# A streamed-weight ring of four buffers instead of five, one more weight block kept resident, and a new order of a step's groups, in a recurrent attention kernel

## The chip, the cores and the metric

The kernel runs on one core of one Trainium2 chip. The metric is the device time of one execution in microseconds (us). The kernel before has a median of 2057.08 us over three runs, from 2056.86 to 2064.43.

## The reference

Two branches read the same `x` of 2048 x 640 and are mixed by a gate.

```python
# branch A: attention with a window of 256 keys, 32 heads of 20
# branch B: 64 segments of 32 tokens, one after the other
for s in range(n_seg):
    h = concatenate([mem, x[segment s]])          # 8 + 32 = 40 tokens of 640
    q = einsum('btd,dhe->bhte', h, Wq)            # 32 heads of 192
    k = einsum('btd,dhe->bhte', h, Wk)
    v = einsum('btd,dhe->bhte', h, Wv)
    p = softmax(mask(q k^T * scale))
    o = einsum('bhte,hed->btd', p v, Wo)
    mem = o[:, :8, :]                             # the next segment needs this
    outs.append(o[:, 8:, :])
return g * a + (1 - g) * b                        # g = sigmoid(x . gate_w)
```

Branch B is a recurrence: segment s+1 needs the first eight rows of segment s. Each of its four weights has 640 x 6144 elements of two bytes, so all four together are read once per segment and don't fit into the on-chip memory at once.

## The kernel before

The kernel computes branch A first (to about 300 us), then what branch B can compute for all segments together, then 64 steps, one for each segment. The steps are what the change touches.

A step works on four groups of eight heads. For each group there are the projections q, k and v, the transposes tq and tk, the scores s, the transposed probabilities p, the values pv and two halves oa and ob of the output projection. `m` turns the new memory rows at the end. `STEP` is the order in which TensorE does them:

```python
STEP = ("k0 q0 k1 tk0 tq0 q1 s0 tk1 q2 tq1 k2 v0 p0 s1 tq2 q3 k3 pv0 tk2 v1 p1 s2 oa0 tq3 tk3 ob0 pv1 v2 p2 s3 oa1 ob1 pv2 v3 p3 "
        "oa2 pv3 ob2 oa3 ob3 m")
```

The weights are cut into 84 blocks: five for each of q, k and v in each group (128 rows of 1536 elements, 384 KB), six for o in each group (128 rows of 1280 elements, 320 KB). Most stay in on-chip memory for the whole run ("resident"). The others are fetched from HBM anew in each step ("streamed"), into a ring of buffers of 1536 elements a row:

```python
RING = 5
STREAMED = {"q": ((1,), (1,), (2,), (1,)),        # for each group, which of its blocks are streamed
            "k": ((0,), (3,), (3,), (3,)),
            "v": ((4,), (0, 4), (0, 3), (3,)),
            "o": ((2,), (2, 5), (0, 3), (2, 5))}
...
ring = wctx.enter_context(tc.tile_pool(name="b_w", bufs=RING))
```

A projection of a group takes its five blocks one after the other, four matmuls for each. A streamed block is one DMA issued from SyncE:

```python
def chunk(kind, s, g):
    ...
    wb = pieces(kind, g)                          # the streamed blocks: a ring buffer and a load each
    def f(kt):
        w = w_of(kind, g, kt, wb)
        for j in range(4):
            nc.tensor.matmul(t[32 * j:32 * j + 32, 0:384], lhsT=tile_of(hT)[:, kt, :], rhs=w[:, j * 384:(j + 1) * 384], ...)
    for kt in range(KT):
        sc.op("PE", 160, 330, lambda kt=kt: f(kt), reads=[hT] + [wb[m] for m in wb if m == kt], ...)
```

The output projection does the same with its blocks, three in oa and three in ob. SyncE issues the loads in the order in which TensorE uses the blocks. The load of block n writes the buffer that block n-5 had, so it waits until TensorE has done the four matmuls of block n-5; a matmul on a streamed block waits for its load.

What is not streamed is loaded once, ahead of the steps:

```python
resident = [...every block that is not streamed...]
early, late, last = resident[:EARLY], resident[EARLY:-LAST], resident[-LAST:]   # EARLY = 24, LAST = 11
```

`early` is loaded during branch A, `late` during the stage between, `last` into buffers that come free before or just after the first step begins.

Of the kernel before, what the change touches and what calls it, by code (L numbers as in the profile page):

```python
# [608 lines left out]
def pe_order(nseg):  # L609

    names = [(w.rstrip("0123456789"), w.lstrip("abcdefghijklmnopqrstuvwxyz")) for w in STEP.split()]
    return [(k, s) + ((int(g),) if g else ()) for s in range(nseg) for k, g in names]


STEP = ("k0 q0 k1 tk0 tq0 q1 s0 tk1 q2 tq1 k2 v0 p0 s1 tq2 q3 k3 pv0 tk2 v1 p1 s2 oa0 tq3 tk3 ob0 pv1 v2 p2 s3 oa1 ob1 pv2 v3 p3 "
        "oa2 pv3 ob2 oa3 ob3 m")


KEPT = {"QT": (1, [P, 12 * L + 64 - L]), "Kz": (1, [P, 4, 2, L]), "Px": (2, [P, 64]), "PTx0": (1, [P, 2, 4, 2, MEM]), "PTx1": (1, [P, 2, 4, 2, MEM]),
# [50 lines left out]
def branch_B(ctx, tc, xin, mem0, weights, ring, c, omg_sb, ga_dram, b_dram, outf, hold, held, rest):  # L670
# [6 lines left out]
    sb = {  # L677
        "w": (RING, [P, PIECE]), "tok": (3, [P, 384]), "vtok": (1, [P, 384]), "K02": (1, [P, 4, 2, L]),
        "PTm": (1, [P, 2, 4, L]), "Pm": (1, [P, 4, SEG]), "xg": (2, [P, 2, 12, MEM]), "xv": (1, [P, 384]), "hT": (2, [P, KT, SEG]),
# [354 lines left out]
    with tc.manual_schedule():  # L1034
        parts = []
        for n in names:
# [10 lines left out]

PARTS = {"oa": range(3), "ob": range(3, 6)}
TURNS = (range(2), range(2, KT))
RING = 5  # L1050
EARLY = 24
LAST = 11
HOLD = 5
DENSE = 8
STREAMED = {"q": ((1,), (1,), (2,), (1,)),
            "k": ((0,), (3,), (3,), (3,)),
            "v": ((4,), (0, 4), (0, 3), (3,)),
            "o": ((2,), (2, 5), (0, 3), (2, 5))}


@with_exitstack
def kernel(
# [31 lines left out]
    allp = [(k, g, m) for k in KINDS for g in range(4) for m in range(6 if k == "o" else 5)]  # L1094
    streamed = [(k, g, m) for k, g, m in allp if m in STREAMED[k][g]]
    weights = Weights(tc, B_Wq, B_Wk, B_Wv, B_Wo, streamed)
# [6 lines left out]
    units = [lambda u=u: weights.load_resident(pre, u, nc.sync) for u in early]  # L1103
    ring = wctx.enter_context(tc.tile_pool(name="b_w", bufs=RING))
    first = {}
# [122 lines left out]
```

## Time and profile before

| what | value |
|---|---|
| median of three runs | 2057.08 us |
| span of the profiled execution | 2060.6 us |
| TensorE matmul busy | 1918.0 us, 93% of the span |
| VectorE, ScalarE, GpSimd busy | 50%, 46%, 35% |
| moved by DMA | 593.83 MB, mean 288 GB/s |
| the step's end (line 977), first to last of 64 | 463.3 to 2052.4 us |
| from issue to landing of a streamed block, least, median, most | 3.3, 4.9, 8.3 us |

The last row but one gives the length of a step: (2052.4 - 463.3) / 63 = 25.22 us. In the profile, PE is TensorE's matmul stream and SP is SyncE, which issues the weight loads. `b_w` is a ring buffer, `w_q`, `w_k`, `w_v`, `w_o` and `hold` are resident blocks, and `in_B_Wq_dram` and the like are the weights in HBM. "Landing" is the moment at which the semaphore of a DMA says that its data is there. In the table of waits, each row is one line of the kernel, what it waited for, the total time in us, how many times, and the longest. A row of a stretch gives the busy time of each engine in it, the granted TensorE clock, the mean busy share of the 16 DMA engines, and the rate in GB/s.

### The profile page before, as it was taken

What the parts mean: (1) busy time and instruction counts of PE and PEld (TensorE: products, weight loads), DVE (VectorE), ACT (ScalarE), POOL (GpSimd) and SP (SyncE); (2) the same over time, 40 slices, a digit from 0 to 9 for tenths busy, and PEclk for the clock granted to TensorE, in tenths of its full rate; (3) what the DMA queues carried; (4) which work ended last, traced back from release to release, by engine and by line L of the source; (5) the groups of instructions that cost most, each with busy time, mean ns of one, the idle gap of its engine ahead of it and who ended that gap; (6) DMA issues with size and microseconds to landing.
All of it is one profiled execution on the core that took longest, in us unless ns stands there. A gap on an engine that the chain in (4) does not pass through costs nothing. (4 is left out here: it accounts for less than half of the span.)

```text
span 2060.6 us, 92206 instructions
## 1 busy us (share of the span) xinstructions
PE 1918.0 (93%) x39670; PEld 1411.6 (69%) x39670; DVE 1027.7 (50%) x3337; ACT 947.3 (46%) x1949; POOL 717.4 (35%) x2008
## 2 busy tenths in 40 slices
PE   7999999989999999999999999999999999999997
PEld 6878878756666666666666666766666666666665
DVE  4888853334444444444444444544444444444444
ACT  3888832334444444444444444444444444444443
POOL 4221121233333333333333333433333333333332
PEclk9999999999999999999999999999999999999999
DMA  4222149789999999999999999999999999999997
GB/s 138 86 82 70 45 99 353 204 271 339 330 327 335 324 334 334 328 328 338 335 329 333 329 327 324 336 321 329 319 337 331 335 334 319 338 332 332 337 329 256
DMA packets 251153, 593.83 MB, mean 288 GB/s; under 512 B 39528, under 2 KB 59120, under 8 KB 250736
## 3 DMA queue, kind: packets, MB, share of 16 engines
q1 hardware_dynamic: 219248, 540.07, 75.2%
q0 software_dynamic: 31488, 47.78, 8.6%
q8 instruction: 313, 5.13, 1.0%
q14 instruction: 104, 0.85, 0.1%
HBM read 558.33 MB, written 29.37 MB: 285 GB/s over the span
## 5 line engine op out<-in xcount | busy, mean ns | idle before, releaser
L773 PEld LDWEIGHTS <-b_hT 128*32 128x32 bf16 x15360 | 374.7, 96 | 261.4 <-issue 65.5
L968 PEld LDWEIGHTS <-b_OT 128*64 128x64 bf16 x6144 | 371.9, 110 | 59.9 <-issue 36.9
L773 PE MATMUL ps_q<-w_q,b_hT 128*32 128x384 bf16 x4096 | 257.6, 329 | 1.6 <-issue 1.6
L773 PE MATMUL ps_k<-w_k,b_hT 128*32 128x384 bf16 x4096 | 246.0, 329 | 0.0
L968 PE MATMUL ps_o<-hold,b_OT 128*64 128x320 bf16 x2560 | 236.5, 300 | 0.0
L968 PE MATMUL ps_o<-b_w,b_OT 128*64 128x320 bf16 x1792 | 206.5, 301 | 26.6 <-DMA b_w<-in_B_Wo_dram 24.5
L919 DVE TENSOR_TENSOR b_PTm<-PT_ps,marks 128x320 bf16<-128x320 f32 x256 | 125.9, 492 | 207.6 <-PE PT_ps L907 207.6
L824 DVE TENSOR_TENSOR b_Kz<-tr_k,marks 128x256 bf16<-128x256 bf16 x256 | 108.0, 422 | 221.2 <-PE tr_k L797 217.2
L773 PE MATMUL ps_v<-w_v,b_hT 128*32 128x384 bf16 x3584 | 212.8, 327 | 0.0
L946 ACT CAST b_OT<-ps_pv 128x480 bf16<-128x480 f32 x256 | 142.9, 558 | 144.9 <-PE ps_pv L942 144.9
L239 ACT ACTIVATE pt<-s_ps 128x1024 bf16<-128x1024 f32 x180 | 183.5, 1025 | 55.2 <-PE s_ps L236 52.0
L784 ACT CAST b_tok<-ps_k 128x384 bf16<-128x384 f32 x256 | 122.4, 478 | 166.2 <-PE ps_k L773 157.6
L784 ACT CAST b_vtok<-ps_v 128x384 bf16<-128x384 f32 x256 | 122.5, 478 | 158.4 <-PE ps_v L773 156.6
L718 POOL DMA_DIRECT2D b_xg<-xin x256 | 141.9, 554 | 83.5 <-POOL b_QT L810 51.4
L968 PE MATMUL ps_o<-w_o,b_OT 128*64 128x320 bf16 x1792 | 170.6, 300 | 0.2 <-ACT b_vtok L784 0.2
L829 POOL COPY b_K<-b_xg 128x64 bf16<-128x64 bf16 x256 | 60.5, 236 | 312.7 <-PE S_ps L853 309.4
L784 ACT CAST b_tok<-ps_q 128x384 bf16<-128x384 f32 x256 | 122.9, 480 | 91.3 <-PE ps_q L773 90.8
L806 ACT COPY b_QT<-tr_q 128x384 bf16<-128x384 bf16 x256 | 123.3, 482 | 85.0 <-PE tr_q L797 85.0
L773 PE MATMUL ps_v<-b_w,b_hT 128*32 128x384 bf16 x1536 | 131.7, 331 | 29.2 <-DMA b_w<-in_B_Wv_dram 28.1
L997 DVE CAST b_hT<-mem_ps 128x16 bf16<-128x16 f32 x126 | 22.5, 178 | 267.6 <-PE mem_ps L991 264.3
L1013 POOL DMA_DIRECT2D out_dram<-b_ga x128 | 63.5, 496 | 246.8 <-DVE b_ga L1009 237.3
L797 PEld LDWEIGHTS <-b_tok 128*64 128x64 bf16 x3072 | 108.2, 110 | 41.6 <-issue 23.3
(141 smaller groups left out, 3720.7 us busy)
## 6 DMA issues: line engine op xcount, KB each, us to landing
b_w<-in_B_Wv_dram SPq DMA_DIRECT2D x384, 384.0 KB, 4.9
b_w<-in_B_Wo_dram SPq DMA_DIRECT2D x448, 320.0 KB, 4.8
b_w<-in_B_Wk_dram SPq DMA_DIRECT2D x256, 384.0 KB, 5.1
b_w<-in_B_Wq_dram SPq DMA_DIRECT2D x256, 384.0 KB, 5.1
xin<-hold POOLq DMA_DIRECT2D x8, 1536.0 KB, 12.2
b_xg<-xin POOLq DMA_DIRECT2D x256, 48.0 KB, 4.5
w_q<-in_B_Wq_dram SPq DMA_DIRECT2D x16, 384.0 KB, 4.3
w_k<-in_B_Wk_dram SPq DMA_DIRECT2D x16, 384.0 KB, 3.7
```

Of the source, the lines that this page charges most:

```text
L239: nc.scalar.activation(out=pt, in_=sp[:], func=ACT.Exp, scale=scale)
L718: sc.op("POOL", 540, 5000, lambda: nc.gpsimd.dma_start(tile_of(b)[:].rearrange("p i b t -> p (i b t)"), xin[s, :, c:c + 192]), writes=[b])
L773: nc.tensor.matmul(t[32 * j:32 * j + 32, 0:384], lhsT=tile_of(hT)[:, kt, :], rhs=w[:, j * 384:(j + 1) * 384], start=(kt == 0), stop=(kt == ...
L784: nc.scalar.copy(dst, src)
L797: nc.tensor.transpose(t[64 * a:64 * a + 64, k, :], tok["tile"][:, c:c + 64], ident[:], tile_position=(0, 64 * a))
L806: nc.scalar.copy(dst, tq["tile"][:].rearrange("p b (j t) -> p b j t", t=SEG))
L824: nc.vector.tensor_tensor(out=tile_of(Kz)[:, :, :, 0:SEG], in0=src, in1=mk_z.unsqueeze(1).unsqueeze(3).to_broadcast([P, 4, 2, SEG]), op=AL ...
L829: nc.gpsimd.tensor_copy(tile_of(K02)[:, :, :, SEG:L], src[:, :, 0::2, :])
L919: nc.vector.tensor_tensor(out=tile_of(PTm)[:], in0=src.to_broadcast([P, 2, 4, L]), in1=mk_m.unsqueeze(1).unsqueeze(3).to_broadcast([P, 2, ...
L946: sc.op("ACT", 560, 50, lambda: nc.scalar.copy(tile_of(OT)[:, 0:12 * L], o["tile"][:, 0:12 * L]), reads=[o], writes=[OT])
L968: nc.tensor.matmul(t[64 * h:64 * h + 64, 0:D // 2], lhsT=OT["tile"][:, c:c + 64], rhs=w, start=(g == 0 and m == 0 and n == 0), stop=(g == ...
L1013: sc.op("POOL", 500, 3000, lambda h=h: nc.gpsimd.dma_start(half(outf, h), mine(tile_of(ga), h)), reads=[ga])
```

## The change

One ring buffer is given up, and in its room one more block is kept resident. So 20 blocks are streamed in a step instead of 21: 13 of q, k and v (before: 14) and 7 of o (as before). Which blocks are streamed is chosen anew, and TensorE does the parts of a step in a new order. The parts themselves are the same. The aim is to read less from HBM in each step without needing more on-chip memory.

```diff
-STEP = ("k0 q0 k1 tk0 tq0 q1 s0 tk1 q2 tq1 k2 v0 p0 s1 tq2 q3 k3 pv0 tk2 v1 p1 s2 oa0 tq3 tk3 ob0 pv1 v2 p2 s3 oa1 ob1 pv2 v3 p3 "
-        "oa2 pv3 ob2 oa3 ob3 m")
+STEP = ("k0 q0 q1 tk0 tq0 k1 s0 tq1 v0 tk1 k2 q2 p0 s1 q3 tk2 pv0 tq2 k3 v1 p1 s2 tq3 oa0 "
+        "tk3 pv1 ob0 v2 p2 s3 oa1 pv2 v3 ob1 p3 oa2 pv3 ob2 oa3 ob3 m")
...
-RING = 5
+RING = 4
...
-STREAMED = {"q": ((1,), (1,), (2,), (1,)),
-            "k": ((0,), (3,), (3,), (3,)),
-            "v": ((4,), (0, 4), (0, 3), (3,)),
-            "o": ((2,), (2, 5), (0, 3), (2, 5))}
+STREAMED = {"q": ((2,), (3,), (3,), (1,)),
+            "k": ((0,), (2,), (3,), (0,)),
+            "v": ((2,), (3,), (3,), (0, 4)),
+            "o": ((0, 3), (0,), (0, 3), (0, 5))}
```

## The prediction, made before the changed kernel ran

> **What bounds the kernel now.** I read first the table of stretches, for the steady part of the 64 steps, then TensorE's waits in the same stretch, then the DMA issues, then the timeline around one load.
>
> ```profile
> core 0: us, PE busy (x) PEld busy (x) DVE busy (x) ACT busy (x) POOL busy (x), PEclk, DMA share, GB/s
> 950.00:1950.00 1000.00, 933.06 (x20866) 668.66 (x20860) 469.97 (x1709) 436.60 (x992) 382.22 (x1112) 1.00 0.96 330
> ```
>
> TensorE is busy 93% at full clock, and the 16 DMA engines 96%. No other engine reaches half. Two resources run close together, so the waits must say which one holds.
>
> ```profile
> engine line waited for: us in total, times, longest us
> PE mem_ps L991 <- ACT b_OT L977: 22.7, 39, 0.8
> PE ps_v L773 <- DMA b_w<-in_B_Wv_dram: 18.9, 35, 1.4
> PE ps_o L968 <- DMA b_w<-in_B_Wo_dram: 10.1, 26, 1.1
> PE ps_k L773 <- DMA b_w<-in_B_Wk_dram: 4.4, 6, 1.3
> PE ps_q L773 <- DMA b_w<-in_B_Wq_dram: 2.8, 6, 1.4
> ```
>
> The first row is the recurrence, once a step, and the change doesn't touch it. The other four are streamed weights that came late: 36.2 us in 1000 / 25.22 = 39.65 steps, 0.9 us a step. This is a lower bound, because modelled ends of matmuls hide part of a wait. So I took the distance from the start of each part to the start of the next in all steps of the trace, and compared its mean with its 5th percentile, which is the pace without a wait. The undisturbed step is **23.33 us**; the real one is 25.22. Of the 1.9 us between them, 1.58 stand in front of streamed blocks and 0.33 elsewhere. Late weights are the only thing that a change of streaming can win back.
>
> ```profile
> b_w<-in_B_Wv_dram SPq DMA_DIRECT2D x237, 384.0 KB, 4.9
> b_w<-in_B_Wo_dram SPq DMA_DIRECT2D x279, 320.0 KB, 4.7
> b_w<-in_B_Wq_dram SPq DMA_DIRECT2D x159, 384.0 KB, 5.2
> b_w<-in_B_Wk_dram SPq DMA_DIRECT2D x158, 384.0 KB, 5.1
> ```
>
> A load takes some 5 us from issue to landing (mean of all, one by one: 4.97). The timeline shows when a load is issued:
>
> ```profile
> 1001.33 0.34 PE L773 MATMUL ps_q<-b_w,b_hT 128*32 128x384 bf16 x4
> ...
> 1001.72 1.46 SPq L517 DMA_DIRECT2D b_w<-in_B_Wv_dram  x2
> ```
>
> The four matmuls end at 1001.67, and 0.05 us later SyncE issues the next load into a freed buffer. This holds at all 21 places of the step: the issue comes 0.04 us after the end of the use five blocks earlier. SyncE never has a free buffer, so **the ring sets when loads start**. A buffer's cycle is 0.04 (issue) + 4.97 (load) + 0.61 (the block lies ready) + 0.38 (use) = 6.0 us, and indeed 21 blocks x 6.0 / 5 buffers = 25.2 us.
>
> **What the skill says.** The Trainium skill, "DMA: Bandwidth & Descriptors", section "Anatomy of one DMA", gives a transfer a fixed part of about 2.0 us, mostly the confirmation of the last byte. The trace has more than this to explain: in the mean the first row of a block starts 2.27 us after the issue, its 128 rows take 1.19 us, and it lands 1.52 us later. A small store in a quiet stretch started its first row after 0.82 us, so some 1.45 us of the load are a queue. The same page, "Issuing engines are not separate DMA queues", says that all queues share the same 16 engines; the trace agrees, with GpSimd's small transfers, of 20 to 96 KB, landing only after 4.4 to 5.1 us at the median. "Perfetto Trace Analysis", section "Optimization Strategy", says that the same gap coming back on the engine that should be saturated can mean too few buffers. Here that is so already with five.
>
> **The change, part by part.**
>
> *Traffic.* A step streams 14 x 384 + 7 x 320 = 7616 KB before and 13 x 384 + 7 x 320 = 7232 KB after. The DMA engines are busy 0.96 x 25.22 = 24.2 us a step, of which the weight queue has a share of 87.7% of the span, 22.1 us. One block is 22.1 x 384 / 7616 = 1.11 us. The DMA engines' work falls from 24.2 to **23.1 us a step**. If DMA throughput were all, and the share stayed 0.96, the step would be 23.1 / 0.96 = 24.1 us.
>
> *New order.* The TensorE parts are the same and the number of changes between the 32-wide and the 64-wide tiles is too: eight stretches of each kind in both orders, and a change costs about 0.1 us. The distances that evacuations need stay long enough. The shortest new one is p2 to pv2 with s3 and oa1 between: 0.06 + 0.33 + 3 x 0.27 = 1.2 us, while VectorE's two products behind p end 0.96 us after its start (1000.48 to 1001.44 in the timeline). So 0 us, and the undisturbed step stays 23.33.
>
> *The ring.* For each streamed block I count its lead: from the end of the use of the block that had its buffer to its own first matmul, at the undisturbed pace (0.162 us a piece of q, k or v, 0.271 of o, both from the timeline). Before, with five buffers: mean 5.18, least 3.98. After, with four: mean 4.29, in order of the step 4.5 4.5 4.7 4.5 4.5 4.7 4.5 4.4 4.4 4.4 4.5 4.7 4.6 4.2 4.3 3.6 3.5 3.7 3.4 4.1. The new places are spread more evenly, but the o blocks at the end have 3.4 to 3.7 us only. A load that takes longer than its lead stops TensorE for the difference, and each stop lengthens the leads of the blocks around it. Walking through the steps with one constant load time gives the stop per step:
>
> | load time, us | 4.0 | 4.2 | 4.3 | 4.4 | 4.5 | 4.6 | 5.0 |
> |---|---|---|---|---|---|---|---|
> | before, 5 buffers | 0.06 | 0.26 | 0.36 | 0.46 | 0.58 | 0.78 | 1.58 |
> | after, 4 buffers | 0.65 | 0.93 | 1.13 | 1.41 | 1.76 | 2.16 | 3.77 |
>
> The row of before meets the trace: at 5.0 us it says 1.58, and 1.58 was measured in front of streamed blocks at a mean load of 4.97. With four buffers the same stop, so the same time as now, comes at a load of 4.45 us. **The change pays only if a load becomes at least 0.5 us shorter.**
>
> *How long a load takes with four buffers.* The 1.45 us of queue can shrink. Sorted by how much weight data stood ahead of a load when it reached the DMA engines, the trace has 4.23 us with less than half a block ahead (26 loads), 4.89 with about 1.1 and 5.57 with about 1.85: 0.93 us for each block ahead, and 1.17 blocks ahead in the mean. One buffer less takes at most one block out of this queue: 4.97 - 0.93 = 4.04 us. If only half of it is felt, because TensorE's pace and not the queue gives way, it is 4.5. I take the middle, **4.27 us**; between the columns of 4.2 and 4.3 this is a stop of 1.07 us. The step is then 23.33 + 0.33 + 1.07 = 24.73 us, 0.49 less than now; times 64 that is 31 us.
>
> *Outside the steps.* The additional resident block is loaded once, about 1.1 us of the DMA engines, and in the stretch of 360 to 440 us their share is 0.71. 0 to 1 us. The sum: 2057 - 31 = **2026 us**.
>
> **The rivals.**
>
> 1. *The latency doesn't give way.* For it: loads issued while only two others were under way still took 4.9 us against 5.1 with four, a weak dependence. If a load keeps 4.97 us, the stop is 3.65 us, the step 27.3 and the time some 2190. Against it: the DMA engines are 96% busy and over a microsecond of the load is waiting in line, which needs loads ahead to wait for.
> 2. *The queue vanishes wholly and TensorE becomes the bound.* For it: the leads are even, and traffic falls by 5% as well. At 4.04 us the stop is 0.69, the step 24.35, the time 2001. Against it: engines whose queue is short run dry now and then, so the share can't stay at 0.96.
> 3. *The new order costs TensorE a wait*, such as pv2 behind VectorE. 0.2 us a step would be 13 us. The trace shows hardly a wait of this kind now.
>
> **Range and chances.** Loads of 4.04 and 4.5 us give 2001 and, with a step of 25.42, about 2070. These are the ends of the range, a little widened for the walk's error below. Faster by over 2% needs a step under 24.58, a load of about 4.2, just under my middle: 0.34. Slower by over 2% needs 4.62 us or rival 3 on top of a long load: 0.13. The rest is within 2%.
>
> **What would show it.** In the changed profile the landing of weights should read 4.1 to 4.4 us at the median. The DMA share in the steps should be 0.92 to 0.95, against 0.96. TensorE's waits should move from v to the o blocks at the step's end, where the leads are shortest. The recurrence should stay at about 0.57 us a step. Landings still near 4.9 would show rival 1, waits on VectorE in pv rival 3. The weakest step is the load time: 0.1 us of it is 0.2 to 0.4 us a step.

## The result, and the profile after

The changed kernel has a median of 2136.96 us over four runs (2123.07 to 2141.07), against 2058.67 us of the kernel before in the same runs: a ratio of 1.0365, 95% interval 1.032 to 1.041. It is 3.65% slower; 2026 us and a range up to 2070 were predicted. The profiled execution is the shortest of the four, and its steps tell where the time went: their end comes at 463.9 us for the first time and at 2113.1 for the 64th, so a step takes (2113.1 - 463.9) / 63 = **26.18 us** instead of 25.22. The part ahead of the steps is as long as before.

The row of the steady stretch, with the columns as before (busy time of each engine, clock, DMA share, GB/s):

```profile
950.00:1950.00 1000.00, 908.39 (x20097) 635.02 (x20096) 448.96 (x1644) 425.93 (x955) 367.65 (x1071) 1.00 0.92 303
```

TensorE is less busy, 91% instead of 93%, and the DMA engines have room, 0.92 instead of 0.96. Both resources became idler and the step longer. That is what waiting for a latency looks like. TensorE's waits in this stretch (line, what it waited for, total us, times, longest):

```profile
PE ps_v L773 <- DMA b_w<-in_B_Wv_dram: 24.0, 45, 1.4
PE mem_ps L991 <- ACT b_OT L977: 21.7, 38, 0.6
PE ps_q L773 <- DMA b_w<-in_B_Wq_dram: 18.9, 30, 1.6
PE ps_o L968 <- DMA b_w<-in_B_Wo_dram: 13.7, 29, 1.3
PE PT_ps L905 <- DVE b_Pm L883: 5.3, 24, 0.4
PE ps_k L773 <- DMA b_w<-in_B_Wk_dram: 3.5, 6, 1.3
```

Late weights cost 24.0 + 18.9 + 13.7 + 3.5 = 60.1 us in 38.2 steps, 1.6 us a step, where it was 0.9. The recurrence (second row) is unchanged. A wait of the transposed probabilities on VectorE is new. The loads themselves did get shorter, as the DMA issues show (last column: median us from issue to landing):

```profile
b_w<-in_B_Wo_dram SPq DMA_DIRECT2D x266, 320.0 KB, 4.2
b_w<-in_B_Wv_dram SPq DMA_DIRECT2D x190, 384.0 KB, 4.3
b_w<-in_B_Wq_dram SPq DMA_DIRECT2D x154, 384.0 KB, 4.6
b_w<-in_B_Wk_dram SPq DMA_DIRECT2D x152, 384.0 KB, 4.3
```

They were 4.7 to 5.2 us. The mean of all, one by one, fell from 4.97 to 4.38 us; 4.27 was predicted. So the load time came out nearly as expected and the time didn't. The experiments ask why.

### The profile page after: what moved, and what is told of

It reads as the page before. It is cut to its first block, busy times and chain, and to the rows that moved or that the text cites. A ratio compares the mean times of both kernels' runs of the same rounds, so it can differ in the third digit from the quotient of the medians.

```text
span 2121.3 us, 91957 instructions
## 1 busy us (share of the span) xinstructions
PE 1932.7 (91%) x39670; PEld 1395.8 (66%) x39670; DVE 1022.2 (48%) x3337; ACT 957.6 (45%) x1949; POOL 717.6 (34%) x2008
## 3 DMA queue, kind: packets, MB, share of 16 engines
q8 instruction: 313, 5.13, 1.0%
## 4 chain that ended last, share of the span: by engine, by line
PE 49%; DMA 41%; DVE 5%; ACT 3%; issue 2%; SPq 0%; POOL 0%; ACTq 0%; POOLq 0%
DMA b_w<-in_B_Wv_dram 14%; DMA b_w<-in_B_Wo_dram 11%; PE ps_o L968 11%; DMA b_w<-in_B_Wq_dram 10%; PE ps_k L773 6%; PE ps_q L773 6%; PE ps_v L773 4%; PE t_psum L584 4%; DMA b_w<-in_B_Wk_dram 3%; PE qk_ps L138 3%; PE t_psv L602 2%; PE tr_k L797 2%; PE s_ps L236 2%; PE S_ps L853 1%; DVE pt L241 1%
## 5 line engine op out<-in xcount | busy, mean ns | idle before, releaser
L968 PEld LDWEIGHTS <-b_OT 128*64 128x64 bf16 x6144 | 359.7, 110 | 71.6 <-issue 42.7
L773 PE MATMUL ps_q<-w_q,b_hT 128*32 128x384 bf16 x4096 | 244.7, 327 | 0.0
L773 PE MATMUL ps_v<-w_v,b_hT 128*32 128x384 bf16 x3840 | 234.1, 327 | 0.0
L773 PE MATMUL ps_k<-w_k,b_hT 128*32 128x384 bf16 x4096 | 234.0, 328 | 0.0
L968 PE MATMUL ps_o<-b_w,b_OT 128*64 128x320 bf16 x1792 | 207.2, 302 | 24.8 <-DMA b_w<-in_B_Wo_dram 24.1
L968 PE MATMUL ps_o<-hold,b_OT 128*64 128x320 bf16 x2560 | 223.5, 301 | 0.0
L773 PE MATMUL ps_v<-b_w,b_hT 128*32 128x384 bf16 x1280 | 109.5, 331 | 47.2 <-DMA b_w<-in_B_Wv_dram 45.7
L873 DVE TENSOR_REDUCE sm<-S_ps 128x4 f32<-128x160 f32 x256 | 82.3, 322 | 121.0 <-ACT S_ps L870 121.0
```

The lines of the kernel that those rows point to most:

```text
L873: nc.vector.tensor_reduce(out=x["sum"][:], in_=view(), axis=AX.X, op=ALU.add)
L968: nc.tensor.matmul(t[64 * h:64 * h + 64, 0:D // 2], lhsT=OT["tile"][:, c:c + 64], rhs=w, start=(g == 0 and m == 0 and n == 0), stop=(g == ...
```

## The experiments

Theory A: what binds is the time of a load against its lead, the room that the ring gives it. Rivals: B, the new order and choice of blocks; C, the throughput of the DMA engines.

### Four buffers alone

```diff
-RING = 5
+RING = 4
```

> The kernel before with four ring buffers and nothing else: its old order, its 21 streamed blocks. Theory A (the ring: the load time and its scatter against the leads, which fall to about 4.1 us): the walk gives a stop of 2.8 to 3.7 us a step at constant loads of 4.4 to 4.6 us, and scatter adds about 1 us, so a step of 27.5 to 28.5 us and 2200 to 2270 us in all, ratio 1.07 to 1.10. Theory B (the new order and choice of blocks cost the time, not the ring): within 15 us of the kernel before. Theory C (DMA throughput: 24.2 us of DMA engine time a step at the share of 0.92 seen with four buffers): a step of 26.3 us, some 2130 us. The landing at the median should be 4.3 to 4.5 us in A.

Measured: 2202.98 us, the mean of 2192.75 and 2213.25, against 2060.16 of before on the same chip, a ratio of 1.069; two further executions (2226.16 and 2231.78 us) were in a slower state with a lower granted clock and are left out. The profiled execution is that of 2213.25 us, with a step of 27.61 us and a DMA share of 0.91. The landing is 4.4 us at the median. This is the low end of A's range. B as the only cause falls: the ring by itself costs 27.61 - 25.22 = 2.39 us a step. C's 2130 us is too low.

### The changed kernel with five buffers

```diff
-RING = 4
+RING = 5
+ALIAS = {('v', 3, 3): ('v', 3, 2)}     # this resident block is left out, its neighbour is read in its place
```

> The changed kernel with five buffers: new order, new choice, 20 streamed blocks. The room for the fifth buffer comes from leaving one resident v block of the last group out, whose matmuls read the neighbouring block instead, so the work of TensorE and the streamed traffic are those of the changed kernel. Theory A: leads rise to 5.4 us, loads of 4.7 to 4.9 us, a stop of 0.3 to 0.9 us, a step of 24.1 to 24.6 us and 1985 to 2020 us in all. Theory B: still slower than before, 2110 to 2135 us. Theory C: 23.1 to 24.1 us of DMA engine time at a share of 0.96, a step of 24.1 to 25.1 us, 1985 to 2050 us.

Measured: 2003.4 us, ratio 0.9703 (0.966 to 0.9745), a step of 24.30 us. This is within the ranges of A and C, and B is out. It isn't a replacement, as it leaves a block of weights out to make room for the fifth buffer. But it shows the parts of the change apart:

| step, us | 21 blocks, old order and choice | 20 blocks, new order and choice |
|---|---|---|
| 5 buffers | 25.22 | 24.30 |
| 4 buffers | 27.61 | 26.18 |

One block less with the new order and choice is worth 0.92 us with five buffers and 1.43 with four. The buffer costs 1.88 us with the new set and 2.39 with the old. The change gave 1.88 for 0.92. Each cell is one execution, and executions of one kernel differ by up to 20 us, 0.3 us a step; by the medians, each against that of the kernel before in the same runs, the buffer costs 2.1 and 2.2 us a step and the new set gives 0.9 and 1.0. The row of the steady stretch with four buffers and the old set:

```profile
950.00:1950.00 1000.00, 874.38 (x18929) 617.16 (x18927) 428.51 (x1548) 396.83 (x900) 346.36 (x1007) 0.99 0.91 300
```

And with five buffers and the new set:

```profile
950.00:1950.00 1000.00, 955.47 (x21625) 677.65 (x21627) 478.90 (x1767) 456.07 (x1027) 397.03 (x1150) 1.00 0.96 327
```

The changed kernel with five buffers asks for fewer bytes a step than the old set with four, and moves more of them in a second, because it does more steps in it. C would allow the 2003 us too; the runs with six buffers and without the small transfers tell A and C apart.

### The new order alone

The kernel before with the `STEP` of the changed kernel, five buffers and the old choice.

> The kernel before with the new order alone: five buffers, the old choice of 21 streamed blocks. Theory A: the leads keep their mean of 5.18 us, the walk gives a stop of 1.6 instead of 1.5 us at 4.97 us, and the new wait of p1 on VectorE that the changed kernel's profile shows adds 0.2 us a step: 2055 to 2080 us. Theory B: 2110 to 2135 us. Theory C: within 10 us of the kernel before.

Measured: 2085.54 us, ratio 1.0129 (1.0072 to 1.0187), a step of 25.53. This is a little above A's range, and the wait on VectorE that was to add 0.2 us isn't among its waits. B's 2110 us and C's 10 us are missed too. In the new order two pairs of the old choice's uses come 0.3 us apart (k3 and v1, ob1 and oa2), where the closest were 0.5 us apart before; that this makes the difference is not shown. The order is no gain by itself.

### Even leads

The kernel before, with 14 and 7 other blocks streamed, so that the least lead is 4.81 us instead of 3.98.

```diff
+STREAMED = {"q": ((), (2, 4), (4,), (3,)),
+            "k": ((0, 4), (1,), (4,), (1,)),
+            "v": ((3,), (1,), (0, 3), (2,)),
+            "o": ((2, 3), (2,), (0, 3, 5), (5,))}
```

> The kernel before with another choice of the same number and sizes of streamed blocks (14 and 7), picked so that the leads with five buffers are even: least 4.81 us instead of 3.98, mean 5.18 as before. Theory A: the stop falls from 1.6 to between 0.6 and 1.0 us, a step of 24.3 to 24.7 us, 2000 to 2025 us in all. Theory C: the bytes and so the DMA engine time are the same 24.2 us a step and the share is 0.96 already, so within 15 us of the kernel before.

Measured: 2096.43 us, ratio 1.0161 (1.0109 to 1.0213), a step of 25.79. A as I had written it failed here: the leads got better and the time worse. C isn't met either, as the same bytes took longer. TensorE's waits say where:

```profile
PE ps_k L773 <- DMA b_w<-in_B_Wk_dram: 35.1, 53, 2.2
PE mem_ps L991 <- ACT b_OT L977: 22.4, 39, 0.6
PE ps_v L773 <- DMA b_w<-in_B_Wv_dram: 10.2, 24, 1.2
```

Two thirds of the waiting for weights is in front of k (35.1 of 53.1 us, with 6.6 for q and 1.2 for o), above all at block 1 of k1. By place in the step, the mean load takes from 4.2 us (block 0 of k0) to 6.2 (block 2 of q1), and 5.8 at k1. The loads of k0's two blocks, of k1 and of the first of q1 are issued as a bunch, within some 2.3 us, and each has more to wait for: if the rows of the weight queue are dealt to the loads in the order of time, the first row of these four comes about 1.4, 2.0, 2.2 and 3.3 us after the issue. **A load's time isn't a number that the choice of blocks leaves alone.**

### The same walk with the loads' own times

This made me repeat the walk of the prediction with times from the traces: once with the mean of all loads, once with the mean of each place in the step, and once with the time of each single load. What is measured is the step less 23.33 + 0.33 us.

| kernel | buffers, blocks | mean load | stop: one mean | stop: mean of each place | stop: each load's own | measured |
|---|---|---|---|---|---|---|
| before | 5, 21 | 4.97 | 1.52 | 0.98 | 1.56 | 1.56 |
| changed | 4, 20 | 4.38 | 1.34 | 1.34 | 2.37 | 2.52 |
| four buffers alone | 4, 21 | 4.45 | 3.12 | 2.94 | 3.83 | 3.95 |
| changed, five buffers | 5, 20 | 4.79 | 0.33 | 0.00 | 0.53 | 0.64 |
| new order alone | 5, 21 | 4.98 | 1.63 | 1.51 | 1.89 | 1.87 |
| even leads | 5, 21 | 5.13 | 0.59 | 1.89 | 2.24 | 2.13 |

With each load's own time the walk meets all six within 0.15 us. So the mechanism, load against lead, is right, and the one constant for all loads was wrong. This is a replay: the times come from the very execution that they reproduce, so it says what late loads cost and not why they are late. Nor are the times independent draws: dealt out at random among the steps, each at its own place, those of the changed kernel make the stop some 0.6 us larger. Around the mean of its place a load scatters by 0.5 to 0.6 us (standard deviation) in these six. A load that is early gains nothing, as the block then lies ready, and one that is late stops TensorE. With four buffers, where mean load and mean lead are nearly the same, this scatter costs 2.37 - 1.34 = 1.03 us a step in the replay; no run changed the scatter alone. In the kernel before it cost 1.56 - 0.98 = 0.58, and the favourable places of its loads gave 1.52 - 0.98 = 0.54 back. That the one mean met the measurement there was two errors of the same size.

### Without the small transfers

GpSimd's four loads of `b_xg` (48 KB each) are left out of the steps but for the first; its data is used throughout.

```diff
-        if (s, g) not in groups:
-            b = groups[s, g] = sc.buf("xg")
+        if not groups:
+            b = groups[0] = sc.buf("xg")
```

> The changed kernel without the loads of b_xg, the four small GpSimd transfers of 48 KB a step (one is made at the start and its data used throughout), which took about 0.9 us of DMA engine time a step. Theory D (with four buffers the time of a load and its scatter bind, not DMA throughput): the load gets shorter by the small share it queued behind these, about 0.1 us, and the step falls by 0.2 to 0.3 us, so 10 to 25 us below the changed kernel, 2110 to 2125. Theory C (DMA throughput binds with four buffers too): the step falls by all of 0.9 us, 2070 to 2085. Theory E (these transfers are what scatters the load times): the scatter of a load falls from 0.5 to below 0.3 us, the stop from 2.4 towards 1.3 us, and the time to 2060 to 2080 with a median load nearly unchanged.

> The same cut in the kernel before (five buffers, 21 blocks). Theory D with DMA throughput binding the kernel before: its 24.2 us of DMA engine time a step fall to 23.3, the load from 4.97 to 4.5 us or so, and the step by 0.6 to 0.9 us: 2000 to 2020 us. If the load time alone binds the kernel before as it does the changed one, the gain is as small as there: 2035 to 2050.

Measured: in the changed kernel 2124.91 us (ratio to before 1.0314, 1.025 to 1.0378) with a step of 26.14; in the kernel before 2042.0 us, ratio 0.9909 (0.9883 to 0.9935), a step of 25.05. In the changed kernel DMA throughput (C) is out, by 40 us. D's time is met with 12 us less, but the two intervals overlap, and the profiled steps differ by 0.04 us instead of 0.2 to 0.3. In the kernel before the gain is that of the load time alone (2035 to 2050 us), not that of throughput (2000 to 2020). The row of its stretch:

```profile
950.00:1950.00 1000.00, 936.51 (x20910) 671.50 (x20905) 469.98 (x1709) 438.12 (x994) 296.25 (x949) 0.99 0.95 324
```

Its DMA engine time is 0.95 x 25.05 = 23.8 us a step against 24.2, so about half of the 0.9 us went, and the step fell by 0.17. That speaks against throughput as the bound of the kernel before, less clearly than in the changed one. Theory E falls: the scatter around the mean of the place is 0.52 us without these transfers and 0.49 with them. What scatters the loads stays open.

### Six buffers

The changed kernel with `RING = 6`; a second resident v block is left out in the same way.

> The changed kernel with six buffers, 20 streamed blocks; the room comes from two resident v blocks left out, whose matmuls read the neighbouring blocks. Leads rise to 6.6 us in the mean, 5.4 at least. Theory D: loads of about 5.3 us hide nearly always, a stop of 0.1 to 0.3 us, a step of 23.8 to 24.1 us, 1965 to 1985 us in all, and the time of a load rises above that of five buffers because more of them queue. Theory C: the DMA engines' 23.1 to 23.7 us a step at a share of 0.97 give 23.8 to 24.4 us, 1965 to 2005.

Measured: 1968.99 us, ratio 0.9559 (0.9508 to 0.961), a step of 23.65. The row of the stretch:

```profile
950.00:1950.00 1000.00, 971.54 (x22232) 691.09 (x22230) 496.90 (x1816) 467.81 (x1055) 403.08 (x1173) 1.00 0.96 335
```

And all of TensorE's waits in it:

```profile
PE mem_ps L994 <- ACT b_OT L980: 24.7, 42, 0.9
PE S_ps L856 <- POOL b_QT L813: 1.0, 1, 1.0
PE ps_pv L938 <- issue: 0.7, 2, 0.5
PE S_ps L856 <- issue: 0.2, 1, 0.2
```

No weight is late any more; what is left is the recurrence. The step is the 23.33 + 0.33 us that the prediction gave for a kernel without stops. The loads take 4.95 us, more than with four buffers though not the 5.3 expected, and a block lies ready for 1.72 us in the mean (0.44 in the changed kernel): that is the reserve that swallows the scatter. And the same DMA share of 0.96 stands here beside 335 GB/s without a wait and in the kernel before beside 330 with 0.9 us of waits a step. A share of 0.96 alone tells nothing of the bound. The time fits theories C and D both; what speaks against C is that at this share no weight is late.

### Half of each load

The changed kernel, four buffers; a streamed block brings half of its columns, and the matmuls read these twice. Half of the weights of each streamed block is left out.

> The changed kernel with four buffers and its 20 loads, each of half the bytes: a streamed block brings 768 (o: 640) of its columns and the matmuls read these twice, so half of each streamed block's weights is left out and TensorE's work is the same. DMA engine time falls to about 13 us a step, so throughput can't bind. Theory D: what is left of a load is its fixed part, 3.2 to 3.6 us, about the least leads of 3.4, so a stop of 0.2 to 1.0 us, a step of 23.9 to 24.7 us and 1975 to 2025 us. If four buffers as such cost the time (a hand-over or an issue each, whatever the size): 2090 to 2130. If a load's time is nearly all bytes and queue: a load of 2 to 2.5 us, no stop, 1955 to 1970.

Measured: 1992.75 us, ratio 0.9676 (0.9624 to 0.9728), a step of 24.13 and a DMA share of 0.64. The issues of the stretch of 800 to 1800 us:

```profile
b_w<-in_B_Wo_dram SPq DMA_DIRECT2D x288, 160.0 KB, 2.5
b_w<-in_B_Wv_dram SPq DMA_DIRECT2D x207, 192.0 KB, 2.6
b_w<-in_B_Wk_dram SPq DMA_DIRECT2D x166, 192.0 KB, 2.6
b_w<-in_B_Wq_dram SPq DMA_DIRECT2D x166, 192.0 KB, 2.9
```

And the waits of the steady stretch that the kernel with six buffers doesn't have:

```profile
PE PT_ps L914 <- DVE b_Pm L892: 7.7, 34, 0.4
PE ps_o L978 <- DMA b_w<-in_B_Wo_dram: 2.8, 4, 0.9
PE ps_v L782 <- DMA b_w<-in_B_Wv_dram: 1.4, 4, 0.5
```

Four buffers as such cost little: with loads of 2.8 us in the mean, below the least lead of 3.4, nearly nothing waits for weights (4.2 us in 41.4 steps, 0.1 us a step). The step is 0.48 us above that with six buffers; 0.19 of this is a wait of p1 on VectorE (7.7 us), of which the next experiment tells, and some 0.2 stay open. D's time is met, but not for its reason: the load is shorter than the 3.2 to 3.6 us that I had put as its fixed part, so more of it is bytes and queue. Half of the bytes relieve the ring and the throughput at once, so this run doesn't tell A from C.

### The new wait on VectorE

In the changed kernel, but not with five or six buffers, the exponential of s1 stands behind the copies of pv0 on ScalarE: the scheduler ranks instructions through the weight loads, so the ring's size reaches ScalarE's order. One term takes this out:

```diff
-o["rank"] = o["dur"] + o["lat"] + max((ops[k]["rank"] for k in o["outs"]), default=0)
+o["rank"] = o["dur"] + o["lat"] + max((ops[k]["rank"] for k in o["outs"] if ops[k]["eng"] != "SP"), default=0)
```

> The changed kernel with one word more in its scheduler: the rank by which ready instructions of ScalarE and VectorE are ordered no longer runs through the weight loads. In the changed kernel the exponential of s1 and of s3 stands behind the copies of pv on ScalarE, with five or six buffers it stands before them; this puts it before them with four buffers too. TensorE's order, the loads and the ring are those of the changed kernel. Theory F (this order, a side effect of the ring's size, is what makes p1 wait on VectorE): the wait of PT_ps on b_Pm goes, 0.15 to 0.3 us a step, so 10 to 20 us below the changed kernel: 2115 to 2128, if the loads don't take it back at once; then 2128 to 2140. If the wait of p1 comes from late loads alone, it stays and so does the time.

Measured: 2135.51 us, ratio to before 1.0365 (1.0305 to 1.0424), as the changed kernel. TensorE's waits, to be compared with those of the changed kernel above:

```profile
PE ps_v L773 <- DMA b_w<-in_B_Wv_dram: 27.9, 52, 1.6
PE mem_ps L991 <- ACT b_OT L977: 21.8, 38, 0.6
PE ps_o L968 <- DMA b_w<-in_B_Wo_dram: 20.5, 33, 1.3
PE ps_q L773 <- DMA b_w<-in_B_Wq_dram: 18.9, 29, 1.5
PE ps_k L773 <- DMA b_w<-in_B_Wk_dram: 5.7, 11, 1.0
```

The wait on `b_Pm` is gone, so the order made it, and the waits for weights have grown from 60.1 to 73.0 us. The loads took back what TensorE gained, as was expected for that case (2128 to 2140 us): the wait lay in the shadow of late weights.

## Why the prediction was wrong, point by point

- **What bounds the kernel: right.** The issue still comes 0.04 us after the use that frees the buffer, at each of the 20 places, and the identity holds: 0.04 + 4.38 + 0.44 + 0.38 = 5.24 us, times 20 blocks / 4 buffers = 26.2.
- **Traffic: the bytes fell as told, the engine time didn't.** 23.1 us of DMA engine time a step were expected; 0.92 x 26.18 = 24.1 were used. With five and six buffers it is 0.96 x 24.30 = 23.3 and 0.96 x 23.65 = 22.7. It wasn't the bound in the changed kernel, where the share had room, nor with six buffers, where no weight was late.
- **New order costs 0 us: right in effect.** The undisturbed step with six buffers is 23.65 us, as summed. The reason given (p2 to pv2) was not where a wait arose; p1 waited (rival 3 in another place: 5.3 us in 38.2 steps, 0.14 us a step), through ScalarE's order, which I hadn't compared. The run without that wait took the same time.
- **The load time: nearly right.** 4.38 us instead of 4.27; the walk turns this into 1.34 instead of 1.07, so 0.27 us a step. The way there was half right: with the rows dealt to the loads in the order of time, the first row comes about 0.35 us earlier than before, and the landing follows the last row about 0.35 us sooner, while the prediction put the whole gain into the queue ahead of the first row. The fixed part of about 2.0 us that the prediction quotes from the Trainium skill, "DMA: Bandwidth & Descriptors", is stated in "Anatomy of one DMA" for transfers issued from GpSimd; SyncE issues these loads, so it need not hold for them.
- **The stop from one constant load time: the step that failed.** The walk took one load time for all loads. At the measured mean it gives 1.34 us, the loads' own times give 2.37, and 2.52 was measured. The missing 1.03 us is scatter, by the replay. The sentence that "the row of before meets the trace" was my proof for it, and one agreement was too little: there the places took off 0.54 and scatter added 0.58.
- **The sum.** 24.73 predicted, 0.27 from the mean and 1.03 from the scatter make 26.03; 0.15 are left to 26.18, about the size of the new wait in this execution. In time, 1.45 us x 64 = 93 us, which makes 2026 into 2119; the profiled execution took 2123.07 us. The 14 us from there to the median of 2137 are between one execution and another, and no trace shows them.
- **Rivals.** Rival 1 (latency stays at 4.97) and rival 2 (the queue vanishes, TensorE binds) both looked at the mean alone. A rival with the right mean and a wrong spread was missing.
- **Where waits would move.** To the o blocks at the end, where leads are shortest: only in part. They are 13.7 of 60.1 us; v has 24.0 and q 18.9. The other three signs came true (landings of 4.2 to 4.6 us at the median, about what was named; a share of 0.92; the recurrence at 0.57 us a step) while the time did not: they tell of the mean load, and none of its spread.

## What to carry to other kernels

When a ring of buffers is refilled as it is used, compare the lead of each load with the whole spread of load times, not with their mean: a late load costs and an early one gains nothing, so a ring with no reserve pays for the scatter at every place. Before trading a buffer for less traffic, look whether the transfers are short of bandwidth or short of time; here loads waited for buffers, and a buffer was worth about twice what the additional resident block, the new order and the new choice gave together. Test a model of the waits on more than one kernel before trusting it: one agreement can be two errors that cancel.

## What the runs showed of the hardware that was not expected

- A load of half the bytes took 2.8 us in the mean against 4.38, less than I had put as the fixed part of any load here.
- A row of 3072 bytes took 121 ns at the median in all kernels that load whole blocks, but 137 ns in the mean before, 144 in the changed kernel and 135 with six buffers; the slowest 1% took 550 to 670 ns or more. With fewer loads under way the rows weren't faster. Why is open.
- The DMA engines moved 335 GB/s with six buffers at the same busy share, 0.96, at which the kernel before moved 330.
